# Loads whose 384-byte pieces are laid at a pitch of 512 bytes in on-chip memory: a gated linear attention with a max-out feed-forward layer on one core

## The chip, the cores and the metric

The kernel runs on one core of one Trainium2 chip. The core has five engines with queues of their own: TensorE (PE, matrix multiply; PEld is its weight load), VectorE (DVE), ScalarE (ACT), GpSimd (POOL) and SyncE (SP), which here only issues transfers. Sixteen DMA engines move data between the chip's main memory and the on-chip memory of 128 partitions. The metric is device time of one execution in microseconds (us), lower is better. A profile is of one execution: its span reaches from the first instruction to the last.

## The reference, cut to what matters

```
f = 1 / (1 + exp(-f_logit))
state = 0                                     # (B, H, D, D)
for t in range(S):
    state = f[:, :, t, :, None] * state + einsum('bhd,bhe->bhde', k[:, :, t], v[:, :, t])
    y[:, :, t] = einsum('bhd,bhde->bhe', q[:, :, t], state)
x = y.transpose(0, 2, 1, 3).reshape(B * S, H * D)
out = maximum(x @ w1, x @ w2) @ w_out
```

B = 4 batches, H = 8 heads, S = 768 positions, D = 48. q, k, v and f_logit have the shape (4, 8, 768, 48) in float32. w1 and w2 are 384 x 1024, w_out is 1024 x 384. The output is 3072 x 384 in float32.

## The kernel before, in words

The work is cut into 12 steps s. Step s covers 256 positions of one batch, all eight heads: `w, b = divmod(s, 4)`. Partition p holds positions 2p and 2p + 1 of the stretch, so a load of one of the four tensors brings, for each partition and each head, two neighbouring rows of 48 floats, which is 384 bytes in one piece of main memory. A load therefore has 128 x 8 = 1,024 pieces, and the 48 loads (f, k, q, v for 12 steps) have 49,152.

`load` (L117 to L126) issues a load from SP. In even steps it is one transfer (L125). In odd steps it is two: heads 3 to 7 go to places 0 to 4 of the slot (L122) and heads 0 to 2 to places 5 to 7 (L123), because odd steps keep their heads turned by three.

All loads land in one tile, `slots` (L113), which has 25 slots of 768 floats, of which the order below uses the numbers 0 to 18. Eight pieces of 384 bytes fill a slot of 3,072 bytes without gaps. The weights land there first: w1 in slots 0 to 3, w2 in 4 to 7, w_out in 8 to 11, each half of a weight in two neighbouring slots, packed without gaps (`staged`, L128; 2 x 3,072 bytes are 3 x 512 floats). Loads of later steps go to the same slots once the weights have been worked up.

Each step turns f into logarithms of the gates and running sums: E, F and G on ACT (L219, L223, L227; E reads the loaded f), e on DVE or POOL, C on PE, X and Z on ACT (L244, L249). Then k and q are scaled: i and j (L253, L257) work on the loaded tiles in place, K and Q (L264, L267) write bfloat16 copies. V (L272 to L275, recorded at the helper's line L109) copies v to bfloat16. PE transposes k and q (L285), multiplies them (L302), applies them to v (L354) and to the carried state (L335, L368). The result x goes out of PSUM to the tile xT; a step M (L422) moves 24 KB within on-chip memory by DMA, so that the heads of a fourth tile fill up three others. The feed-forward layer uses max(a, b) = b + relu(a - b): d (L430) multiplies x by w1 - w2, r takes the relu (L439, L441), and o (L451, L454) adds x times w2 w_out and the relu times w_out. Step O stores the output from SP (L473).

The order of all this is written out by hand in the string ORDER, one word per action, read from left to right (L569). A word such as `Lv7s@1` means: load v of step 7 from SP to slot 1. Every engine works its words in that order, and waits where data or a buffer is not ready. On SP the loads, the steps M and the stores stand in one queue, and so a load that waits for its slot holds up what is behind it.

Where `slots` lies follows from the tiles allocated before it. The program has 16,512 bytes in each partition before its first pool. The pool of constants behind it has, in bytes per partition: tri 256, u_inc 256, ones2 4 (given 32), e 2 x 1,024, kp and qp 3 x 2,048 each, vb 4 x 2,048, st 8 x 1,024, ident 256, perm 1,280, fill 768, mask 512, wd and wo 6,144 each, and m2 2,304: together 48,672. So `slots` begins at byte 16,512 + 48,672 = 65,184 of each partition.

Of the kernel before, what the change touches and what calls it, by code (L numbers as in the profile page):

```python
# [11 lines left out]
F32 = mybir.dt.float32  # L12
# [46 lines left out]
def kernel(  # L59
# [15 lines left out]
    B, H, S, D = q.shape  # L75
    C = 128
# [7 lines left out]
    d_ff = moe_w1.shape[1]  # L84
    FG = d_ff // C
    KT = HD // C
# [9 lines left out]
    inp = ctx.enter_context(tc.tile_pool(name="inp", bufs=1))  # L96
# [13 lines left out]

    slots = inp.tile([C, 25, H * 2 * D], F32, name="slots")  # L113
    loaded = {s: {} for s in range(n_s)}
    sources = {"f": f_logit, "k": k, "q": q, "v": v}

    def load(nm, s, slot):  # L117
        w, b = divmod(s, B)
        src = sources[nm][b, :, w * W:(w + 1) * W, :].rearrange("h (p two) d -> p h (two d)", two=2)
        dst = slots[:, slot, :].rearrange("p (h x) -> p h x", h=H)  # L120
        if s % 2:
            nc.sync.dma_start(out=dst[:, 0:H - TURN, :], in_=src[:, TURN:H, :])  # L122
            nc.sync.dma_start(out=dst[:, H - TURN:H, :], in_=src[:, 0:TURN, :])  # L123
        else:
            nc.sync.dma_start(out=dst, in_=src)  # L125
        loaded[s][nm] = slots[:, slot, :].rearrange("p (h two d) -> p h two d", h=H, two=2)  # L126

    def staged(i):  # L128
        return slots[:, i:i + 2, :].rearrange("p s x -> p (s x)")

    HF = d_ff // 2
    w1_f, w2_f = ([staged(i + 2 * h).rearrange("p (k m) -> p k m", k=KT) for h in range(2)] for i in (0, 4))
    wo_f = [staged(8 + 2 * h).rearrange("p (f m) -> p f m", m=HD) for h in range(2)]

    def load_rows(dst, w, e, h):
# [24 lines left out]
    for nm, n_bufs, shape in (("e", 2, [C, H, DP]), ("kp", 3, [C, 2, H, DP]),  # L160
# [3 lines left out]
        for i in range(n_bufs):  # L164
            t = consts.tile(shape, BF16, name=f"{nm}{i}")
# [17 lines left out]
    for i, (kt, blk) in enumerate(meets):  # L183
        for r in range(2):
            for head, n, at0, first in ((tiles[kt][r], D, 0, 0), (tiles[KT][r], GAP, D, takes[r][kt] * GAP)):
                row = head * D + first
                lo, hi = max(row, blk * C), min(row + n, (blk + 1) * C)
                if lo < hi:
                    x = r * DP + at0 + lo - row
# [17 lines left out]


    def flat(t):
        return t.rearrange("p h two d -> p (h two d)")  # L210

    def by_parity(t):
        return t.rearrange("p h two d -> p two h d")
# [3 lines left out]
    def step_E(s):  # L217
        gate[s] = work.tile([C, H, 2, D], F32, name="gate", tag="gate", bufs=2)
        nc.scalar.activation(flat(gate[s]), flat(loaded[s]["f"]), AF.Exp, bias=0.0, scale=-1.0)  # L219

    def step_F(s):
        ell[s] = work.tile([C, H, 2, D], F32, name="ell", tag="ell", bufs=2)
        nc.scalar.activation(flat(ell[s]), flat(gate[s]), AF.Ln, bias=1.0, scale=1.0)  # L223
# [311 lines left out]
    def store_wd(q, e, b):  # L535
        src = banks[:, b:b + 2, :].rearrange("p b x -> p (b x)")[:, 0:KT * QF]
        copy(e, wd[:, :, q * QF:(q + 1) * QF], src.rearrange("p (k m) -> p k m", k=KT))

    steps = {
        "Lf": lambda s, e, b: load("f", s, b), "Lk": lambda s, e, b: load("k", s, b),  # L540
        "Lq": lambda s, e, b: load("q", s, b), "Lv": lambda s, e, b: load("v", s, b),
        "Wa": lambda i, e, b: load_rows(w1_f, moe_w1, e, i),
        "Wb": lambda i, e, b: load_rows(w2_f, moe_w2, e, i),
# [58 lines left out]
```

## Time and profile before

| | |
|---|---|
| median of three runs | 143.67 us (143.39 to 143.99) |
| the profiled execution | 144.36 us |
| its span | 142.6 us |
| PE busy | 122.4 us, 86% |
| DVE, ACT, POOL busy | 96.6, 88.8, 63.2 us |
| DMA | 56,281 packets, 29.15 MB |
| granted TensorE clock | full throughout |

The page of the profile cuts the span into 40 slices of 3.56 us and gives for each the busy tenths of every engine, the busy share of the DMA engines and the rate in GB/s. The "chain that ended last" goes back from the last instruction, at each step to what released it. The groups of instructions give a count, the busy time and the mean of one. A view of the DMA alone can be asked for any window of the span; it gives the number of packets that began in the window and the mean rate. For 384-byte packets a rate converts to time by 16 engines x 384 bytes / rate: 261 GB/s is 23.5 ns for each packet on each engine.

### The profile page before, as it was taken

How to read it: one execution, taken by the hardware profiler on the slowest of the kernel's cores; microseconds unless marked ns; L12 is line 12 of the kernel's file. 1: busy time of each engine (PE TensorE's matmuls, PEld its weight loads, DVE VectorE, ACT ScalarE, POOL GpSimd, SP SyncE). 2: the span in 40 equal slices, each digit the busy share in tenths (PEclk: the TensorE clock that was granted, in tenths of full speed). 3: DMA queues.
4: the chain of work that ended last, by engine and by line, in shares of the span. 5: the costliest groups of instructions: out<-in, count | busy, mean ns of one | idle time of the engine just before them, and what ended most of it. 6: DMA issues, size and time to landing. Idle time of an engine off the chain costs nothing.

```text
span 142.6 us, 5440 instructions
## 1 busy us (share of the span) xinstructions
PE 122.4 (86%) x2335; PEld 89.7 (63%) x2335; DVE 96.6 (68%) x188; ACT 88.8 (62%) x131; POOL 63.2 (44%) x69
## 2 busy tenths in 40 slices
PE   0145369998999899989996999999999999999992
PEld 0033358796656577756655866597766776668661
DVE  5869978748998879648553976975996864510321
ACT  3666243798969897975976669397848261235210
POOL 7110763952296748249982047569935200000000
PEclk9999999999999999999999999999999999999999
DMA  4999999999999976998869989379910350105023
GB/s 114 268 259 267 381 387 380 315 237 268 265 260 258 225 197 171 231 278 218 250 170 241 280 241 240 86 185 300 318 40 25 115 228 5 28 0 222 5 95 126
DMA packets 56281, 29.15 MB, mean 204 GB/s; under 512 B 50945, under 2 KB 53313, under 8 KB 56257
## 3 DMA queue, kind: packets, MB, share of 16 engines
q1 hardware_dynamic: 56128, 28.76, 76.0%
q8 instruction: 18, 0.29, 0.9%
q10 hardware_dynamic: 128, 0.05, 0.1%
q14 instruction: 7, 0.05, 0.1%
HBM read 23.59 MB, written 4.72 MB: 199 GB/s over the span
## 4 chain that ended last, share of the span: by engine, by line
PE 58%; DMA 13%; ACT 10%; DVE 6%; SPq 4%; POOL 3%; issue 3%; DVEq 0%; ACTq 0%; POOLq 0%
PE banks L454 16%; PE banks L430 16%; DMA slots<-in_v_dram 9%; PE banks L451 7%; PE banks L302 4%; PE banks L354 4%; DMA xT<-xT 4%; ACT vb L109 3%; PE banks L285 3%; DVE qp L267 2%; SPq L125 2%; PE banks L368 2%; POOL e L230 1%; PE banks L335 1%; PE banks L530 1%
## 5 line engine op out<-in xcount | busy, mean ns | idle before, releaser
L430 PE MATMUL banks<-xT,wd 128*128 128x256 bf16 x288 | 34.8, 273 | 1.7 <-DMA xT<-xT 1.6
L454 PE MATMUL banks<-wo,gT 128*128 128x384 bf16 (+2 forms) x200 | 35.3, 320 | 0.0
L310 DVE TENSOR_TENSOR at_m<-banks,mask 128x1024 bf16<-128x1024 f32 x24 | 28.7, 1219 | 6.5 <-PE banks L302 6.3
L430 PEld LDWEIGHTS <-wd 128*128 128x128 bf16 x288 | 26.8, 98 | 6.3 <-DMA xT<-xT 2.1
L439 ACT ACTIVATE gT<-banks 128x1024 bf16<-128x1024 f32 x19 | 19.0, 1024 | 12.6 <-PE banks L430 12.6
L454 PEld LDWEIGHTS <-gT 128*128 128x128 bf16 x200 | 19.3, 98 | 12.0
L109 DVE COPY ob<-banks 128x384 f32<-128x384 f32 (+4 forms) x28 | 9.2, 375 | 13.7 <-PE banks L454 9.5
L109 ACT CAST xT<-banks 128x1024 bf16<-128x1024 f32 (+2 forms) x13 | 11.2, 879 | 9.7 <-PE banks L354 8.7
L264 POOL TENSOR_TENSOR kp<-slots,inv 128x768 bf16<-128x768 f32 x9 | 16.4, 1826 | 1.8 <-ACT inv L244 0.8
L253 POOL TENSOR_TENSOR slots<-slots,one 128x384 f32<-128x384 f32 x9 | 9.4, 1050 | 14.8 <-ACT one L227 9.6
L451 PE MATMUL banks<-m,xT 128*128 128x384 bf16 (+2 forms) x75 | 15.9, 321 | 0.0
L109 POOL CAST vb<-slots 128x768 bf16<-128x768 f32 (+1 forms) x8 | 8.5, 1058 | 12.9 <-DMA slots<-in_v_dram 12.7
L109 DVE COPY trs<-banks 128x2048 bf16<-128x2048 bf16 x10 | 12.1, 1221 | 3.0 <-PE banks L285 2.9
L109 ACT COPY ob<-banks 128x384 f32<-128x384 f32 (+1 forms) x13 | 5.9, 468 | 12.9 <-PE banks L454 12.9
L302 PE MATMUL banks<-trs 48*64 48x128 bf16 x384 | 10.5, 235 | 3.5 <-DVE trs L109 1.5
L219 ACT ACTIVATE gate<-slots 128x768 f32<-128x768 f32 x12 | 10.1, 841 | 3.5 <-DMA slots<-in_f_logit_dram 3.5
L109 ACT CAST vb<-slots 128x768 bf16<-128x768 f32 (+1 forms) x16 | 10.6, 674 | 2.5 <-DMA slots<-in_v_dram 2.2
L302 PEld LDWEIGHTS <-trs 48*64 48x64 bf16 x384 | 7.2, 115 | 7.2 <-issue 3.1
L389 POOL TENSOR_TENSOR st<-tmp_s,dec 128x192 bf16<-128x192 f32 x12 | 6.8, 574 | 10.0 <-DVE tmp_s L384 9.9
L441 DVE TENSOR_SCALAR gT<-banks 128x1024 bf16<-128x1024 f32 x5 | 6.0, 1221 | 6.6 <-PE banks L430 6.6
L267 DVE TENSOR_TENSOR qp<-slots,dec 128x768 bf16<-128x768 f32 x9 | 10.3, 1148 | 0.3
L223 ACT ACTIVATE ell<-gate 128x768 f32<-128x768 f32 x12 | 10.1, 844 | 0.5
(69 smaller groups left out, 170.4 us busy)
## 6 DMA issues: line engine op xcount, KB each, us to landing
out_dram<-ob SPq DMA_DIRECT2D x11, 384.0 KB, 4.2
slots<-in_moe_w_dram SPq DMA_DIRECT2D x4, 768.0 KB, 8.5
slots<-in_f_logit_dram SPq DMA_DIRECT2D x6, 384.0 KB, 6.2
slots<-in_k_dram SPq DMA_DIRECT2D x6, 384.0 KB, 5.7
slots<-in_q_dram SPq DMA_DIRECT2D x6, 384.0 KB, 6.1
slots<-in_v_dram SPq DMA_DIRECT2D x6, 384.0 KB, 6.2
slots<-in_moe_w_out_dram SPq DMA_DIRECT2D x2, 768.0 KB, 14.6
slots<-in_f_logit_dram SPq DMA_DIRECT2D x6, 240.0 KB, 5.6
```

What stands on the lines that cost most here:

```text
L109: (nc.scalar.copy if e == "a" else engines[e].tensor_copy)(out, in_)
L219: nc.scalar.activation(flat(gate[s]), flat(loaded[s]["f"]), AF.Exp, bias=0.0, scale=-1.0)
L223: nc.scalar.activation(flat(ell[s]), flat(gate[s]), AF.Ln, bias=1.0, scale=1.0)
L253: engines[e].tensor_mul(even, even, one[s])
L264: engines[e].tensor_mul(pad("kp", s)[:, :, :, 0:D], by_parity(loaded[s]["k"]), both(inv[s]))
L267: engines[e].tensor_mul(pad("qp", s)[:, :, :, 0:D], by_parity(loaded[s]["q"]), both(dec[s][:, 0:HD].rearrange("p (h d) -> p h d", h=H)))
L302: nc.tensor.matmul(out=ps[h * HC:(h + 1) * HC, j % 2, par, :], lhsT=t[rows, h, 0, j, par, :], rhs=t[rows, h, 1, j].rearrange("p a t -> p ( ...
L310: nc.vector.tensor_mul(at[s][:, jj].rearrange("p r j a t -> p (r j) (a t)"), banks[:, b:b + 2, :].rearrange("p r (j x) -> p (r j) x", j=2) ...
L430: nc.tensor.matmul(out=ps[:, f, :], lhsT=wd[:, kt, ff * C:(ff + 1) * C], rhs=x_flat(g)[:, kt, :], start=(kt == 0), stop=(kt == KT - 1))
L439: nc.scalar.activation(dst, src, AF.Relu)
L451: nc.tensor.matmul(out=ps, lhsT=x_flat(g)[:, kt, cols], rhs=m2[:, kt, m], start=(kt == 0), stop=False)
L454: nc.tensor.matmul(out=ps, lhsT=gT[g][:, ff, cols], rhs=wo[:, ff, m], start=False, stop=(ff == FG - 1))
```

## The change

The tile becomes 19 slots of 8 x 128 floats. Head h's 96 floats go to the first 96 of the 128 places of its part, so that the pieces lie 512 bytes apart instead of 384. A slot grows from 3,072 to 4,096 bytes, the tile from 76,800 to 77,824 bytes, and tiles allocated behind it move up by 1,024 bytes. A half weight is still packed without gaps, in the first 6,144 of the 8,192 bytes of its two slots. The instructions that read the loaded tiles step over the gaps: K, Q, V, i and j go from head to head by 128 floats instead of 96, and E, which read 768 floats in a row, reads eight runs of 96. No instruction, transfer, wait or slot number is added, removed or moved; each transfer keeps its pieces, its source addresses and its place in SP's queue.

```
-    slots = inp.tile([C, 25, H * 2 * D], F32, name="slots")
+    slots = inp.tile([C, 19, H, C], F32, name="slots")
...
         src = sources[nm][b, :, w * W:(w + 1) * W, :].rearrange("h (p two) d -> p h (two d)", two=2)
-        dst = slots[:, slot, :].rearrange("p (h x) -> p h x", h=H)
+        dst = slots[:, slot, :, 0:2 * D]
...
-        loaded[s][nm] = slots[:, slot, :].rearrange("p (h two d) -> p h two d", h=H, two=2)
+        loaded[s][nm] = dst.rearrange("p h (two d) -> p h two d", two=2)
 
     def staged(i):
-        return slots[:, i:i + 2, :].rearrange("p s x -> p (s x)")
+        return slots[:, i:i + 2, :, :].rearrange("p s h x -> p (s h x)")[:, 0:KT * d_ff // 2]
...
     def flat(t):
-        return t.rearrange("p h two d -> p (h two d)")
+        return t.rearrange("p h two d -> p h (two d)")
```

## The prediction

> **What bounds the kernel now.** The change touches only where loads write, so I read first how busy the DMA engines are and when, then the chain that ended last, then the rate of the loads in short windows.
>
> The page of before, busy tenths and queues:
>
> ```profile
> span 142.6 us, 5440 instructions
> ...
> PE   0145369998999899989996999999999999999992
> ...
> DMA  4999999999999976998869989379910350105023
> ...
> DMA packets 56281, 29.15 MB, mean 204 GB/s; under 512 B 50945, under 2 KB 53313, under 8 KB 56257
> ## 3 DMA queue, kind: packets, MB, share of 16 engines
> q1 hardware_dynamic: 56128, 28.76, 76.0%
> ## 4 chain that ended last, share of the span: by engine, by line
> PE 58%; DMA 13%; ACT 10%; DVE 6%; SPq 4%; POOL 3%; issue 3%; DVEq 0%; ACTq 0%; POOLq 0%
> ```
>
> Of the packets, 49,152 are the 384-byte pieces that the change moves. A slice is 3.56 us: the DMA engines are full from the second slice to the fourteenth (to 50 us), PE from the seventh (21 us) on. The chain in order of time shows where a load holds the end:
>
> ```profile
> 2.75 6.09 DMA slots<-in_v_dram
> 8.86 0.84 ACT vb L109
> ...
> 60.10 7.23 DMA slots<-in_v_dram
> 67.35 0.84 ACT vb L109
> ...
> 71.14 5.01 DMA xT<-xT
> 76.16 0.05 issue
> 76.20 4.76 PE banks L430 x42
> ```
>
> So 6.1 us at the start and 7.2 us at 60 us belong to loads, and a step M's transfer takes another 5.0 us behind loads in the same queue. From 76.2 us on the chain is nearly all PE, which is never idle between 80 and 130 us. A change of load time can therefore count only up to 76 us.
>
> The DMA alone, in windows 2.8 to 3.8, 4.9 to 7.9 and 15 to 25 us (the last is nearly all weights):
>
> ```profile
> DMA packets 863, 0.33 MB, mean 325 GB/s; under 512 B 863, under 2 KB 863, under 8 KB 863
> ...
> DMA packets 2072, 0.78 MB, mean 261 GB/s; under 512 B 2072, under 2 KB 2072, under 8 KB 2072
> ...
> DMA packets 2098, 3.83 MB, mean 383 GB/s; under 512 B 78, under 2 KB 737, under 8 KB 2095
> ```
>
> The first load runs at 325 GB/s (16 x 384 / 325 = 18.9 ns for a packet on each engine). From the second one on the pace is 261 GB/s (23.5 ns). The same pieces at the same kind of addresses have two paces, so something other than their addresses makes the 4.6 ns between them.
>
> **The change, part by part.** First, what it does to the write addresses. The tile begins at byte 65,184 of a partition (the sum of the tiles ahead of it), and 65,184 = 254 x 256 + 160. If partitions begin at a multiple of 256, a pitch of 512 puts every piece at 160 past a multiple of 256, not on it. Such a piece covers bytes 160 to 544 and touches three blocks of 256 bytes. Before, the pitch of 384 put even places at 160 (three blocks) and odd places at 32 (bytes 32 to 416, two blocks). The change therefore does not do what its words say: blocks touched go from 2.5 for a piece on average to 3. Packets (49,152) and bytes stay.
>
> What a third block costs can be looked for inside before, since the two transfers of an odd step have different shares of three-block pieces: places 0 to 4 have three in five, places 5 to 7 have one in three. Counting the 384-byte packets in order, the kernel's sixth load (k of step 1) has its five-place part in 9.55 to 10.35 us and its three-place part in 10.5 to 10.9; the seventh (q) has them in 11.05 to 11.85 and 12.0 to 12.4:
>
> ```profile
> DMA packets 558, 0.21 MB, mean 265 GB/s; under 512 B 558, under 2 KB 558, under 8 KB 558
> ...
> DMA packets 268, 0.10 MB, mean 254 GB/s; under 512 B 268, under 2 KB 268, under 8 KB 268
> ...
> DMA packets 559, 0.21 MB, mean 265 GB/s; under 512 B 559, under 2 KB 559, under 8 KB 559
> ...
> DMA packets 270, 0.10 MB, mean 256 GB/s; under 512 B 270, under 2 KB 270, under 8 KB 270
> ```
>
> The part with more three-block pieces is not slower: 265 against 255 GB/s (23.2 against 24.1 ns), with 261 for whole loads at one in two. If the third block made up the whole 4.6 ns, the five-place parts would take 18.9 + 0.6 x 9.2 = 24.4 ns and the three-place parts 22.0. The order is the other way. I take 0 ns for a third block, because these rows measure the very thing; the ends for the range are +4.6 ns (all pieces become like the dear half: 18.9 + 9.2 = 28.1) and -4.6 ns (all run at 18.9).
>
> Next, the readers. K, Q, V, i and j already read runs of 48 floats with steps between them, and only the step from head to head grows. E changes from 768 floats in a row to eight runs of 96, 12 times. The nearest rows, by form:
>
> ```profile
> L219 ACT ACTIVATE gate<-slots 128x768 f32<-128x768 f32 x12 | 10.1, 841 | 3.5 <-DMA slots<-in_f_logit_dram 3.5
> L109 ACT CAST vb<-slots 128x768 bf16<-128x768 f32 x8 | 6.6, 830 | 2.2 <-DMA slots<-in_v_dram 2.2
> ```
>
> The cast of v reads the same 768 floats as 16 runs of 48 and takes 830 ns against 841 in a row. I take 0, with 12 x 11 ns = 0.13 us either way as bounds. The cast's output type differs, but a cost of a run would show with 16 of them. No cover is needed for a cost of nothing.
>
> Last, what does not move: no instruction, wait or queue position changes, SP's queue included. A half weight still fills its two slots from the first byte; the w_out rows now reach from one slot into the other differently, but the casts that free them come, in the written order, ahead of the first loads there, and no wait is added. The other tiles move up by 1,024 bytes, four times 256, so their place against blocks of 256 stays.
>
> The sum: 0 for the writes, 0 for the readers, 0 for waits. The profiled execution took 144.36 us, a span of 142.6 and 1.76 around it; the forecast for it is 144.4. That execution is 0.69 above the median of the runs, so for the runs I give the median, 143.7 us.
>
> **A rule that speaks against it.** The Trainium skill, "DMA: Bandwidth & Descriptors", section "How a descriptor splits into AXI transactions", says that a transaction must start at a multiple of 256 bytes, and that the bytes fetched ahead of an unaligned start still cost beats of 32 bytes. It says so of reads; taken over to the writes here, a piece at 160 would cost 8 + 8 + 1 = 17 beats and one at 32 would cost 8 + 5 = 13, so the mean would go from 15 to 17 and 23.5 ns would become an estimated 26.6. By that rule the sum would be about +1 us (the five first loads, 5 x 64 x 3.1 ns). The windows above do not bear it out for writes.
>
> **The rivals.** A measurement of this kernel can tell about 0.5%, here 0.7 us, from no change.
>
> *B, slower: crossing a third block costs time once the queue is deep.* For it: the loads stand at 261 GB/s from 4.9 us to the weights and again from 37 to 40 us, and that pace needs some cause. Against it: the windows of the odd steps. Price at its upper end, 4.6 ns for a packet, 64 packets of a load on each engine, 0.29 us for a load. The fourth load is 1.2 us late and ACT waits for it already; the fifth is 1.5 us late, and E of step 1 waited for it (0.2 us idle ahead of it at 10.4 us). The sixteenth (v of step 3), whose packets end at 38.7 us, would be 4.7 us late; landing takes 0.9 us more (the fourth load's packets end at 7.9 us, its cast starts at 8.86), and its cast starts at 41.79, a slack of 2.1 us; 2.6 us are left. So +1.5 to +2.6, 145.2 to 146.3 us; I name 145.6. It decides from about 2.2 ns for a packet on (five loads x 64 x 2.2 ns = 0.7 us). The skill's rule above would be a case of it.
>
> *C, faster: equal places suit the writes.* If the write side prefers one phase for all pieces, or if partitions do not begin at a multiple of 256 and the words of the change come true, the deep-queue pace becomes the first load's. For it: 325 GB/s is reached with such pieces. Against it: the layout, and that the 325 were reached with both phases mixed. The fourth load comes 1.2 us earlier, but ACT sat idle only 0.69 us ahead of its cast; the fifth adds the 0.2 us. Around 75 us, PE's idle 1.57 us ahead of its work at 76.2 could go too. So -0.7 to -2.3, 141.4 to 143.0; I name 142.5.
>
> **How the numbers follow.** A, no change: 0.56. B: 0.28; a place whose cause is not known (the two paces) can hide a dependence that two parts of a load do not show. C: 0.16. The predicted time is A's 143.7, its own range 143.0 to 144.4. The range runs into B up to 146.0 (above that some 0.06) and into C down to 142.2 (below that some 0.08). Faster 0.16, same 0.55, slower 0.29, the last with a small part of A's upper tail.
>
> **What would show it.** The three windows at the start: 325, then 261 GB/s after as before for A; about 220 GB/s (16 x 384 / 28.1) at B's upper end; over 300 for C. The cast of v of step 0 starts at 8.86 us in A, near 10 in B, near 8.2 in C. E's mean stays at 841 ns and the cast's at 830. 49,152 packets of 384 bytes remain; more packets than 56,281 would mean that pieces are split, which I have not priced. The prediction is wrong if the write's place changes the pace in the deep queue, or if a gap between the pieces keeps something from being joined that the trace of before does not show.

## The result: 4.8% slower

The changed kernel takes 150.81 us (149.30 to 153.29, four runs) against 143.62 (143.39 to 143.99): a ratio of 1.048, 95% interval 1.040 to 1.055. Two further runs gave 151.20 and 151.76 us; the ratio leaves out the two slow ones of the six (151.76 and 153.29). The prediction was 143.7 with a range of 142.2 to 146.0, so it was wrong, and the time lies even above the dear end of its rival B. The profiled execution of the changed kernel took 149.3 us, the lowest of the four, with a span of 147.5: 4.9 us more than the span of before.

The page of the changed kernel, busy tenths, granted clock, the queue of the loads and the chain by engine:

```profile
span 147.5 us, 5440 instructions
...
PE   0024479998995989989997999999999999999992
...
PEclk9999999999998699999999999999999999999999
DMA  4999999999999999899996999969970070005013
...
q1 hardware_dynamic: 56128, 28.76, 89.5%
## 4 chain that ended last, share of the span: by engine, by line
PE 56%; DMA 16%; SPq 13%; ACT 6%; DVE 3%; issue 2%; POOL 2%; ACTq 0%; DVEq 0%; POOLq 0%
```

The same 56,128 packets and 28.76 MB fill 89.5% of the 16 engines' span, after 76.0%. PE has a new hole in the thirteenth slice (44 to 48 us). The chain has more DMA (16%, was 13%) and far more of SP's queue (13%, was 4%).

The DMA alone, in windows 2.8 to 3.8, 4.9 to 7.9 and 17 to 22 us of the changed kernel:

```profile
DMA packets 796, 0.30 MB, mean 301 GB/s; under 512 B 796, under 2 KB 796, under 8 KB 796
...
DMA packets 1731, 0.65 MB, mean 218 GB/s; under 512 B 1731, under 2 KB 1731, under 8 KB 1731
...
DMA packets 959, 1.92 MB, mean 384 GB/s; under 512 B 31, under 2 KB 31, under 8 KB 957
```

The loads in the deep queue fell from 261 to 218 GB/s: 16 x 384 / 218 = 28.2 ns for a packet on each engine, 4.7 more than 23.5. Weights, whose write addresses keep their place against blocks of 256 bytes, run at 384, against 386 in the same window before. The chain in order of time, with loads and steps M:

```profile
9.91 5.82 DMA slots<-in_q_dram
...
39.70 5.64 DMA slots<-in_v_dram
45.41 0.84 ACT vb L109
...
65.46 7.25 DMA slots<-in_v_dram
72.73 0.84 ACT vb L109
...
76.56 4.52 DMA xT<-xT
81.13 4.76 PE banks L430 x42
```

A load holds the chain at 45.4 us, where before the cast of v of step 3 started at 41.79 with its data there. From 81.13 on the work is that of 76.20 before, 4.9 us later, the whole difference of these two spans.

The readers, by form, cost what they did (841 and 830 ns before):

```profile
L219 ACT ACTIVATE gate<-slots 128x768 f32<-128x768 f32 x12 | 10.1, 843 | 4.3 <-DMA slots<-in_f_logit_dram 4.3
L109 ACT CAST vb<-slots 128x768 bf16<-128x768 f32 x8 | 6.6, 830 | 5.2 <-DMA slots<-in_v_dram 5.2
```

### The profile page after: what moved, and what is told of

Same layout as the page of the kernel before. It is cut to its first block, busy times and chain, and to the rows that moved or that the text cites. A ratio compares the mean times of both kernels' runs of the same rounds, so it can differ in the third digit from the quotient of the medians.

```text
span 147.5 us, 5440 instructions
## 1 busy us (share of the span) xinstructions
PE 124.9 (85%) x2335; PEld 90.9 (62%) x2335; DVE 95.7 (65%) x188; ACT 89.4 (61%) x131; POOL 60.3 (41%) x69
## 3 DMA queue, kind: packets, MB, share of 16 engines
q1 hardware_dynamic: 56128, 28.76, 89.5%
## 4 chain that ended last, share of the span: by engine, by line
PE 56%; DMA 16%; SPq 13%; ACT 6%; DVE 3%; issue 2%; POOL 2%; ACTq 0%; DVEq 0%; POOLq 0%
PE banks L454 16%; PE banks L430 16%; DMA slots<-in_v_dram 9%; PE banks L451 7%; SPq L122 5%; DMA slots<-in_q_dram 4%; PE banks L354 4%; PE banks L302 3%; SPq L125 3%; SPq L123 3%; DMA xT<-xT 3%; PE banks L285 2%; PE banks L530 2%; ACT vb L109 2%; PE banks L335 1%
## 5 line engine op out<-in xcount | busy, mean ns | idle before, releaser
L454 PE MATMUL banks<-wo,gT 128*128 128x384 bf16 (+2 forms) x200 | 36.0, 324 | 0.0
L454 PEld LDWEIGHTS <-gT 128*128 128x128 bf16 x200 | 19.6, 99 | 12.6 <-issue 1.0
L439 ACT ACTIVATE gT<-banks 128x1024 bf16<-128x1024 f32 x19 | 19.0, 1024 | 12.5 <-PE banks L430 12.5
L451 PE MATMUL banks<-m,xT 128*128 128x384 bf16 (+2 forms) x75 | 16.4, 329 | 0.0
L109 DVE COPY trs<-banks 128x2048 bf16<-128x2048 bf16 x10 | 12.1, 1221 | 3.8 <-PE banks L285 3.7
L109 POOL CAST vb<-slots 128x768 bf16<-128x768 f32 (+1 forms) x8 | 6.4, 804 | 16.2 <-DMA slots<-in_v_dram 16.0
L219 ACT ACTIVATE gate<-slots 128x768 f32<-128x768 f32 x12 | 10.1, 843 | 4.3 <-DMA slots<-in_f_logit_dram 4.3
L234 PE MATMUL banks<-e,u_inc 128*128 128x384 bf16 x12 | 4.2, 356 | 7.9 <-DVE e L230 7.5
L223 ACT ACTIVATE ell<-gate 128x768 f32<-128x768 f32 x12 | 10.1, 843 | 0.5
L389 POOL TENSOR_TENSOR st<-tmp_s,dec 128x192 bf16<-128x192 f32 x12 | 6.1, 508 | 8.9 <-DVE tmp_s L384 7.4
```

The costliest lines, as they stand in the source:

```text
L109: (nc.scalar.copy if e == "a" else engines[e].tensor_copy)(out, in_)
L439: nc.scalar.activation(dst, src, AF.Relu)
L451: nc.tensor.matmul(out=ps, lhsT=x_flat(g)[:, kt, cols], rhs=m2[:, kt, m], start=(kt == 0), stop=False)
L454: nc.tensor.matmul(out=ps, lhsT=gT[g][:, ff, cols], rhs=wo[:, ff, m], start=False, stop=(ff == FG - 1))
```

## The experiments

Theory 1: a write pays for every block of 256 bytes that it touches, and the change puts all pieces on three blocks instead of half of them. Theory 2: the gap between neighbouring pieces costs, wherever they lie. Theory 3: a touched block costs by the 32-byte beats up to the end of the piece.

### Where the tile begins, with and without gaps

The edit is a pad, a tile that nothing uses, at the end of the constants, in the kernel of before or in the changed one; 24 floats for "at 0", 32 for "at 32", 56 for "at 128", 16 for "at 224":

```
     m2 = consts.tile([C, KT, HD], BF16, name="m2")
+    pad0 = consts.tile([C, 24], F32, name="pad0")
```

The layout of before at 0:

> The layout of before (pieces 384 bytes apart), with 96 bytes left free ahead of the tile of loads, so that it begins at 65,280 = 255 x 256. Pieces begin at 0 and 128 past a multiple of 256 and touch two blocks each; weights of 2,048 bytes touch eight blocks instead of nine; the tiles behind it, the output's among them, begin at a multiple of 256 too. Theory 1 (a write costs 28.2 / 3 = 9.4 ns for every block of 256 bytes that it touches, however little of it): loads in the deep queue at 18.8 ns for a packet on each engine (326 GB/s, 23.5 ns and 261 GB/s before), weights at 75 ns (435 GB/s, 385 before), time 140 to 142 us. Theory 2 (it is the gap between the pieces that costs, since neighbouring pieces can no longer be joined): as before, 261 GB/s, 143.6 us.

Measured, the DMA in the window 4.9 to 7.9 us:

```profile
DMA packets 2578, 0.97 MB, mean 325 GB/s; under 512 B 2578, under 2 KB 2578, under 8 KB 2578
```

The changed layout at 0:

> The changed kernel (pieces 512 bytes apart) with the same 96 bytes ahead, so that every piece does begin at a multiple of 256. Theory 1 (blocks touched): two blocks each, 326 GB/s, the same time as the layout of before with the 96 bytes, 140 to 142 us. Theory 2 (gaps): 218 GB/s as in the changed kernel, 150 to 151 us.

Measured in the same window:

```profile
DMA packets 2578, 0.98 MB, mean 325 GB/s; under 512 B 2578, under 2 KB 2578, under 8 KB 2578
```

The changed layout at 32:

> The changed kernel with 128 bytes ahead: every piece begins at 32 past a multiple of 256 and covers 32 to 416, two blocks. Weights (nine blocks), output and the steps M touch as many blocks as before, so only the loads differ. Theory 1: 326 GB/s for the loads, 385 for the weights, 141 to 143 us. Theory 2: 218 GB/s, 150 to 151 us. Theory 3 (blocks count by the beats up to the end of the piece: 13 here, 17 at 160): 28.2 x 13 / 17 = 21.6 ns, 285 GB/s, 142 to 143 us.

Measured in the same window:

```profile
DMA packets 2581, 0.97 MB, mean 325 GB/s; under 512 B 2581, under 2 KB 2581, under 8 KB 2581
```

The layout of before at 32:

> A control: the layout of before with 128 bytes ahead. Even places begin at 32, odd ones at 160, so the mix of two and three blocks is that of before with the places exchanged. All theories: 261 GB/s, 143.6 us within 0.5%. A difference would say that moving the tiles does something of its own.

Measured in the same window:

```profile
DMA packets 2073, 0.78 MB, mean 261 GB/s; under 512 B 2073, under 2 KB 2073, under 8 KB 2073
```

The changed layout at 128:

> The changed kernel with 224 bytes ahead: every piece covers 128 to 512, two blocks. Theory 1 (each block touched costs the same): 18.8 ns, 326 GB/s. Theory 2 (gaps): 28.2 ns, 218 GB/s. Theory 3 (beats up to the end, 16 against 17 at 160): 26.5 ns, 231 GB/s.

Measured in the same window:

```profile
DMA packets 2574, 0.97 MB, mean 325 GB/s; under 512 B 2574, under 2 KB 2574, under 8 KB 2574
```

The changed layout at 224:

> The changed kernel with 64 bytes ahead: every piece covers 224 to 608, three blocks, of the first of which only 32 bytes. Theory 1: 28.2 ns, 218 GB/s, as in the changed kernel. Theory 2: the same. Theory 3 (19 beats against 17): 31.5 ns, 195 GB/s.

Measured in the same window:

```profile
DMA packets 1733, 0.65 MB, mean 218 GB/s; under 512 B 1733, under 2 KB 1733, under 8 KB 1733
```

All six together:

| layout | piece covers (bytes past a multiple of 256) | blocks | ns | time against before |
|---|---|---|---|---|
| before at 0 | 0 to 384, 128 to 512 | 2, 2 | 18.9 | 0.987 (0.979 to 0.995) |
| changed at 0 | 0 to 384 | 2 | 18.9 | 0.986 (0.978 to 0.993) |
| changed at 32 | 32 to 416 | 2 | 18.9 | 0.989 (0.982 to 0.995) |
| changed at 128 | 128 to 512 | 2 | 18.9 | 141.15 us, one run |
| before at 32 | 32 to 416, 160 to 544 | 2, 3 | 23.5 | 1.004 (1.000 to 1.008) |
| changed at 224 | 224 to 608 | 3 | 28.2 | 150.9 us, one run |

Theory 2 falls: with gaps and without, at 0, the pace is 325 GB/s. Theory 3 falls: the pieces at 128 and at 160 differ by one beat and take 18.9 and 28.2 ns, those at 160 and at 224 by two and take the same. Only the number of touched blocks sorts the rows, and the mixed layouts lie halfway (18.9 + 28.2 is twice 23.5). A begin on a multiple of 256 is not needed; 32 and 128 do as well. The 18.9 ns of two blocks is also the pace at which the first load runs in every layout, three-block ones too, so these runs do not show what holds a two-block piece there, its reading or its writing.

Theory 1's figures for larger pieces do not come out. At 0 the window 17 to 22 us, mostly weights, moves 402 GB/s in the layout of before, against 386 for the kernel before and an expected 435. That window holds other pieces too. From 15.5 to 18.5 us, nearly all w1 and w2 in pieces of 2,048 bytes, it is 380 against 386: eight blocks instead of nine gave these pieces nothing. What is shown of blocks is shown for the pieces of 384 bytes.

### The tiles behind, alone

```
     slots = inp.tile([C, 25, H * 2 * D], F32, name="slots")
+    pad1 = inp.tile([C, 24], F32, name="pad1")
```

> The layout of before, the 96 bytes behind the tile of loads: loads and weights write where they did, only the tiles behind (x, output) begin at a multiple of 256. An output transfer's pieces of 3,072 bytes then read 12 blocks instead of 13, the 512-byte pieces of the steps M two instead of three. Theory 1: loads 261 GB/s, weights 385; 3,072-byte pieces 113 ns instead of 122; time 143.0 to 143.6 us, since the outputs are mostly beside other work. Theory 2: 143.6 us.

The ratio is 0.999 (0.994 to 1.004). The median 3,072-byte packet takes 121 ns against 122, not 113: reading 12 blocks of on-chip memory instead of 13 gave nothing. So the gain of the layouts at 0 comes from what is written to the tile, loads and weights; the layout at 32, which leaves weights and outputs on as many blocks as before, has the same ratio within its interval, and so it is mostly the loads'.

### Cheap and dear loads in turn

```
-        dst = slots[:, slot, :, 0:2 * D]
+        at = (slot % 2) * 24
+        dst = slots[:, slot, :, at:at + 2 * D]
```

> The changed kernel, with the pieces of a slot with an odd number 96 bytes further on, at a multiple of 256: whole loads of two-block pieces stand between whole loads of three-block pieces. The first eight loads go to slots 12, 13, 14, 15, 16, 12, 17, 18, so 3, 2, 3, 2, 3, 3, 2, 3 blocks. Theory 1, with a packet's record showing the read side, which runs ahead of the write side by some 20 packets on each engine until it is held up: the pace shows the number of blocks, but late: it changes about 20 of a load's 64 packets after the load begins, so a load after a dear one begins at 28.2 ns and goes over to 18.8 within, and the other way round. The same without the lag: 28.2 and 18.8 change at the boundaries of the loads. Theory 2: 28.2 throughout.

Loads of two-block pieces are called cheap here, those of three-block pieces dear. The one run took 145.28 us. Counted in order, the packets of the second load (cheap) begin between 3.68 and 5.08 us, those of the third (dear) between 5.08 and 6.69. The DMA in the windows 3.7 to 4.1 and 4.5 to 5.0, then 5.1 to 5.4 and 6.0 to 6.6:

```profile
DMA packets 239, 0.09 MB, mean 221 GB/s; under 512 B 239, under 2 KB 239, under 8 KB 239
...
DMA packets 423, 0.16 MB, mean 321 GB/s; under 512 B 423, under 2 KB 423, under 8 KB 423
...
DMA packets 254, 0.09 MB, mean 316 GB/s; under 512 B 254, under 2 KB 254, under 8 KB 254
...
DMA packets 345, 0.13 MB, mean 218 GB/s; under 512 B 345, under 2 KB 345, under 8 KB 345
```

The cheap load begins at the dear pace and the dear one at the cheap pace; each goes over to its own after 16 to 24 of its 64 packets on each engine. The pace that the trace shows of a packet is thus that of a write some 20 packets earlier; the reading is that a packet's record shows its read, which runs so far ahead of the writes. Two further things fit. The changed kernel's loads leave 18.9 ns at about the 60th packet of each engine, those of before at about the 84th. A lead of 20 or 17 packets builds up in that time, if reads take 18.8 ns and writes 28.2 or 23.5 (60 x (1 - 18.8 / 28.2) = 20; 84 x (1 - 18.8 / 23.5) = 17).

The windows that the prediction leaned on, moved by that lead, say the opposite. Of the kernel before, for the sixth and seventh load: 9.5 to 9.8 and 11.0 to 11.3 us show the writes of three-place parts, 10.1 to 10.7 and 11.5 to 12.1 those of five-place parts.

```profile
DMA packets 223, 0.08 MB, mean 277 GB/s; under 512 B 223, under 2 KB 223, under 8 KB 223
...
DMA packets 406, 0.15 MB, mean 250 GB/s; under 512 B 406, under 2 KB 406, under 8 KB 406
...
DMA packets 227, 0.08 MB, mean 279 GB/s; under 512 B 227, under 2 KB 227, under 8 KB 227
...
DMA packets 409, 0.15 MB, mean 252 GB/s; under 512 B 409, under 2 KB 409, under 8 KB 409
```

That is 22.1 ns for one three-block piece in three and 24.5 for three in five, which are the 22.0 and 24.4 that the prediction worked out for a dear third block, and then took to be refuted.

### Which loads cost the time

The changed kernel, with the pieces of the later steps 96 bytes further on, which leaves the start on three blocks; with `(s < 2)` in place of `(s > 1)` the pieces of the first two steps move, and the later loads stay on three:

```
-        dst = slots[:, slot, :, 0:2 * D]
+        at = 24 * (s > 1)
+        dst = slots[:, slot, :, at:at + 2 * D]
```

> The changed kernel, in which only the eight loads of steps 0 and 1 write three blocks a piece (at 160 past a multiple of 256); the 40 later loads are put 96 bytes further on and write two. Weights, x and output lie as in the changed kernel. Windows: 218 GB/s up to the weights, 326 after them. Theory 1 with lateness that adds up in the one queue: the fourth load lands at 10.3 us as in the changed kernel, the last weights at 31.0; the loads behind them gain 9.4 ns x 64 = 0.6 us each, and v of step 3 (the eighth behind the weights) lands near 31.0 + 8 x 1.2 + 0.9 = 41.5 us against 45.3 in the changed kernel and 40.3 in before. Time 0.5 to 1.5 us above before, 144 to 146 us. If instead the start's lateness reached the end in full (+2.5 us at the last weights): 146 to 147.

> The other part: the eight loads of steps 0 and 1 write two blocks a piece, the 40 later ones three. Windows: 326 GB/s up to the weights, 218 after them. The last weights land near 27 us, v of step 3 near 27.2 + 8 x 1.8 + 0.9 = 42.5 us; up to the last load of step 7 the queue loses 4.7 ns x 64 = 0.3 us a load against before. Theory 1 with lateness that adds up in the queue: 145 to 147 us, more than the kernel with the dear start, since more loads lie behind the weights than ahead of them and no slack of the start helps them. If the start alone mattered: 142 to 143 us.

> The changed kernel once more beside the two parts, on the same chip: 149 to 151 us, 218 GB/s in the deep queue, v of step 3 landing at 45.3 us. All theories.

With the start on three blocks: 0.999 (0.995 to 1.003), less than expected. With the later loads on three: 1.025 (1.019 to 1.031), somewhat more than expected. The changed kernel again: 1.046 (1.038 to 1.054). In the window 37 to 40 us, behind the weights, the DMA moves 303 GB/s with the dear start (326 expected) and 220 with dear later loads (218 expected). The layouts at 0 and at 32 reach 297 to 316 there, so pieces of two blocks stay somewhat below the 325 of the start; why is not shown. The first casts of v after the weights, with the wait ahead of them in brackets, stand in ACT's timeline. In the kernel before (the cast of step 3 begins at 41.79, within this line):

```profile
40.60 2.57 ACT L109 CAST vb<-slots 128x768 bf16<-128x768 f32 x4
```

With the dear start:

```profile
41.09 2.57 ACT L109 CAST vb<-slots 128x768 bf16<-128x768 f32 x4
```

With dear later loads:

```profile
40.58 1.38 ACT L109 CAST vb<-slots 128x768 bf16<-128x768 f32 x2
42.46 1.37 ACT L109 CAST vb<-slots 128x768 bf16<-128x768 f32 x2 [0.50 <-DMA slots<-in_v_dram]
```

In the changed kernel:

```profile
43.55 1.37 ACT L109 CAST vb<-slots 128x768 bf16<-128x768 f32 x2 [1.14 <-DMA slots<-in_v_dram]
45.41 1.38 ACT L109 CAST vb<-slots 128x768 bf16<-128x768 f32 x2 [0.49 <-DMA slots<-in_v_dram]
```

By the landing events, v of step 3 lands at 40.3 us before, 41.2 with the dear start (41.5 expected), 42.4 with dear later loads (42.5 expected) and 45.3 in the changed kernel. Lateness does add up along SP's one queue, and it passes on once the slack at these casts, about 1.5 us, is used up. A dear start alone is made good, against the kernel before, by cheap loads behind it.

## Why the prediction was wrong, point by point

**What bounds the kernel.** Right for the profiled execution: the DMA is the bound up to about 50 us, and all of the loss came before PE's unbroken stretch (76.2 became 81.13 us). That load time can count "only up to 76 us" did not hold in general: in a second profile of the changed kernel, with a span of 149.8 us, a load of q holds the chain from 82.35 to 88.78, and PE's work on the chain goes on at 92.03.

**The write addresses.** Right: the tile begins 160 past a multiple of 256 and the change raises the blocks touched from 2.5 to 3. The pads change nothing but the begin of the tiles, and the pace followed it. The 160 is a sum of tiles and stands in no trace; but with whole blocks no other multiple of 32 gives the changed layout three blocks a piece with 0 and 64 bytes ahead and two with 96, 128 and 224.

**The price of a third block, 0 ns.** This step failed. It measured 4.7 ns in the mean over the pieces (23.5 to 28.2), just above the upper end of 4.6 that the text kept. Two readings led away from it. The windows of the odd steps were taken as paces of the writes of those parts, while the records run some 20 packets ahead; a part has 40 or 24 on each engine. So the window of a five-place part was about half, and that of a three-place part mostly, of the other part's writes: a half of each gives 23.2 ns (22.0 and 24.4), which is what the five-place windows showed, and 20 in 24 of five-place writes give 24.0, against 24.1 shown. And the 325 GB/s of the first load was taken as a sign that "something other than their addresses" made the two paces; by the runs above it was the time in which reads could run ahead, and the pace behind it was the addresses' own: with two blocks for every piece, the loads stay at 325 GB/s from 4.9 to 7.9 us.

**Rival B.** Its mechanism was right; the text gave it 0.28. Its sum was too small: 1.5 to 2.6 us, against 4.9 between the profiled spans and 7.2 between the medians. The slack at the cast of v of step 3 was about 1.5 us, not 2.1: its load landed at 40.33, 1.6 us after the last of its packets by count, where the fourth load took 0.9; why the landings behind the weights come later is not shown. The cast came 3.6 us later instead of 2.6. And the sum ended there, at the sixteenth load. Behind it the lateness grew: the cast of v of step 7 came 5.4 us later (67.35 to 72.73). Two things are in that. On the chain of this profile, 1.5 us of the growth is PE at a lower clock between 47 and 51 us (see the last section). But with dear later loads alone, at full clock, the cast of step 3 came 0.7 us later (42.46), that of step 7 2.9 (70.24) and the end of the span 3.7 (146.3): the loads behind the sixteenth count.

**The rule that spoke against it** had the direction. The Trainium skill, "DMA: Bandwidth & Descriptors", section "How a descriptor splits into AXI transactions", counts, for reads, a begun block before an unaligned start in full beats but the leftover at the end by its bytes. The measured paces (28.2 ns at 160 where its 17 beats gave an estimate of 26.6 in the mean; 18.9 at 32 and at 128) do not follow the leftover's bytes: in these writes of 384 bytes a last block costs as much as a whole one.

**Readers and order.** Right: 843 and 830 ns, no new wait in the program. **Rival C** named the gain that a true alignment has (0.987, about 142 us), but the change did not have it.

## What to carry to other kernels

For small pieces, count the blocks of 256 bytes that each DMA piece touches from the address at which the tile really begins, not from its offset in the tile: 96 bytes of padding ahead of the unchanged layout made it 1.3% faster, while a pitch of 512 bytes without them made it 4.8% slower. When a pace in a trace changes, ask whether the first part was only a buffer filling; and before two windows are compared, test how far the records run ahead of what limits them. Lateness in a queue has to be summed to the last transfer of the full stretch, not to the first place where it shows.

## What the runs showed of the hardware that was not expected

With the queue full, the cost of a write of 384 bytes goes by the blocks of 256 bytes that it touches: 18.9 ns for two and 28.2 for three. The pace in the records is ahead of the writes by about 17 to 20 packets of 384 bytes (6.5 to 7.7 KB) on each engine.

The granted clock can fall behind a short hole in PE's work. In the profile of the changed kernel PE stands partly idle at 44 to 48 us, with no gap between matmuls longer than 0.95 us, and the clock then falls (windows of 2 us from 44, 46, 48 and 50; the third last column is the clock):

```profile
44.00:46.00 2.00, 0.98 (x35) 0.52 (x33) 1.01 (x2) 1.48 (x3) 2.00 (x2) 1.00 1.32 223
46.00:48.00 2.00, 1.41 (x64) 1.25 (x63) 0.54 (x2) 1.60 (x3) 0.67 (x1) 0.76 1.28 221
48.00:50.00 2.00, 2.00 (x15) 0.95 (x10) 1.92 (x4) 1.94 (x3) 1.50 (x2) 0.50 1.35 225
50.00:52.00 2.00, 2.00 (x39) 1.16 (x40) 0.58 (x2) 0.67 (x3) 0.99 (x1) 0.89 1.28 219
```

At 0.50 the chain's eight matmuls of L454 took 1.94 us where they take 1.30 elsewhere; with L285 and L451 ahead of them it is 3.98 us against 2.46 before. The dip shows in all three profiles of kernels whose loads all touch three blocks (0.71 to 0.78 at 46 to 48 us, 0.50 at 48 to 50), and in no other profile. That the hole causes it is likely by the order of time, but was not tried. It does not explain the loss: of the changed kernel's runs, three at a mean clock of 0.997 to 1.000 took 150.78 to 151.20 us, longer than the profiled one at 0.988 with 149.30.

The two halves on three blocks alone seem to sum to less than the whole: by the ratios to before, and against the 0.989 of the layout at 32, they cost 1.1% and 3.7%, and all loads together 5.8 to 6.0%. The difference is about 1%, and the intervals of the ratios are too wide to say that it is there. Nor is it settled why the medians lie 7.2 us apart where the two profiled spans are 4.9 apart; the profiled execution of the changed kernel was its fastest, and its runs spread over 4 us.
